# A recurrent transformer's segment loop on one core: transposed scores, sums by a ones matmul, V in two column tiles, memory rows copied per PSUM bank

## The chip, the cores and the metric

The kernel runs on one core of one Trainium2 chip. The metric is the device time of one execution in microseconds (us). The kernel before takes 1736.54 us (median of 3 runs, 1736.03 to 1736.92).

The engines are PE (TensorE, matmuls; PEld is its weight load, which overlaps), DVE (VectorE), ACT (ScalarE), POOL (GpSimd) and SP (SyncE, which issues DMAs). Matmuls write into eight PSUM banks, `pb[0]` to `pb[7]`; DVE or ACT copies the results ("evicts" them) to SBUF. PE can run at a reduced clock; the profile records the clock that was granted, 1.00 being full.

## The reference

The output is a mixture of two models, `g*a + (1-g)*b`, over 2048 tokens of width 512. Model b is a linear-memory attention, which the kernel computes first, in about the first 350 us. Model a is the expensive one. It is recurrent: 64 segments, and each needs the memory that the one before produced.

```python
M, seg, H, Dh = 8, 32, 32, 128          # 8 memory rows, 32 tokens, 32 heads of 128
mask = (idx[:, None] < M) | (idx[:, None] >= idx[None, :])
mem = mem0
for s in range(64):
    h = concatenate([mem, x[:, s*32:(s+1)*32]])           # 40 rows x 512
    q, k, v = h@Wq, h@Wk, h@Wv                            # 32 heads each
    p = softmax(where(mask, q@k.T * scale, -1e9))         # 40 x 40 per head
    o = (p @ v) @ Wo                                      # 40 x 512
    mem = o[:8]                                           # needed by segment s+1
    outs.append(o[8:])
```

No work of segment s+1 that depends on `h` can start before the end of segment s, so the loop is one long chain. Anything in a segment that leaves PE idle is paid 64 times.

## The kernel before

The program is scheduled by hand: each engine executes its instructions in the order in which the Python code puts them out, and semaphores follow from declared reads and writes. `L` = 40 rows, `C` = 4 contraction chunks of 128, `E` = 128, `SEG` = 32. In a segment, tokens stand in columns 0 to 31 and memory rows in columns 32 to 39.

```python
# scores: [q, k] per head, 32 matmuls; exp on ACT, mask on POOL, sum / reciprocal / multiply on DVE
ins = pe.matmul(pb[b][0:L, ...], QT_sb[:, h*L:(h+1)*L], KT_sb[:, h*L:(h+1)*L], start=True, stop=True)
... a.activation(P_sb[0:L, h0:h1, :], pb[b][0:L, ...], ACT.Exp, scale=SCALE)
... g.affine_select(P_sb[0:SEG, h0:h1, 0:SEG], ...)
... dv.tensor_reduce(rsum, P_sb, AX.X, ALU.add); dv.reciprocal(rrec, rsum); dv.tensor_tensor(Pn_sb, P_sb, rrec, ALU.mult)

# P has to be turned for P@V: 32 PE transposes, then a DVE copy
ins = pe.transpose(dst, Pn_sb[0:L, h, :], ident[0:L, 0:L])

# V: 8 groups of 512 columns; the output fills only 40 of 128 PSUM partitions
for c in range(c0, c1):
    ins = pe.matmul(pb[vb][0:L, 0:512], hTc[:, c, :], Wv_sb[:, c, 512*j:512*(j+1)], start=(c == 0), stop=(c == C-1))

seq = [("K",0),("K",1),("K",2),("hx",None),("Q",0),("Q",1),("Q",2),("V",0),("sc",0),("sc",1),("V",1),("sc",2),
       ("V",2),("V",3),("V",4),("ptr",0),("V",5),("V",6),("ptr",1),("V",7),("ptr",2)]
... # then P@V (32 matmuls) into OT_sb, evicted by ACT

# output projection: 128 matmuls into ONE bank, then two DVE copies, one after the other
for c in range(C):
    ... pe.matmul(pb[6][:, c*L:(c+1)*L], Wo_sb[:, h, c*128:(c+1)*128], OT_sb[:, h*L:(h+1)*L], ...)
... dv.tensor_copy(aT_st[...], pb[6] columns 0:SEG)            # tokens, "aT"
... dv.tensor_copy(hTc[:, :, SEG:L], pb[6] columns SEG:L)      # memory rows, "hm": K of the next segment waits for this
```

Every fourth segment a finished block of 128 output rows is combined with model b (`brow`, `atr`, `t1`, `fin`) and sent out; `fin` reads bank 6 too.

The softmax here doesn't subtract the row's maximum and nothing guards it: scores larger than these inputs give would overflow.

## Time and profile before

| what | number | where to read it |
|---|---|---|
| PE busy over the span of 1731.7 us | 89% | page, part 1 |
| PE busy between 1000 and 1700 us | 671.39 of 700 us, clock 0.99 | windows |
| first K matmul of the segment loop | 352.3 us | the line's instructions |
| the loop | 1731.7 - 352.3 = 1379.4 us | |
| distance between memory copies (62 intervals, 382.1 to 1707.1 us) | 21.37 us | the line's instructions |

The page's first part (busy us, share of the span, instructions):

```profile
PE 1547.3 (89%) x37477; PEld 1163.0 (67%) x37573; DVE 725.5 (42%) x1733; ACT 732.3 (42%) x1471; POOL 204.1 (12%) x396
```

That average mixes model b with the loop. The windows view, one stretch of the loop only (from:to in us, its length, busy time of each engine, granted clock, DMA share, GB/s):

```profile
1000.00:1700.00 700.00, 671.39 (x16771) 516.14 (x16801) 271.19 (x607) 271.09 (x524) 60.41 (x131) 0.99 0.02 5
```

So the loop is bound by PE, and every other engine has room. The chain of waits shows what PE does in one plain segment (start us, length us, what; L822 is K and Q, L888 V, L874 the transposes, L937 P@V, L950 the output projection):

```profile
1000.74 0.29 DVE aT_st L956
1001.04 0.11 DVE hT L806
1001.14 0.05 issue
1001.19 6.58 PE pb L822 x256
1007.77 0.97 PE pb L888 x4
...
1010.41 2.60 PE pb L888 x12
1013.01 0.40 PE pb L874 x12
...
1016.91 0.71 PE pb L937 x24
...
1018.06 3.59 PE pb L950 x128
```

The V projection alone is 7.2 of these 20.9 us. The group lines tell why it is worth attacking (line, engine, operation, tiles, shapes, count | busy us, mean ns | idle before it):

```profile
L888 PE MATMUL pb<-Wv_sb,hT 128*40 128x512 bf16 x2048 | 498.7, 381 | 4.3 <-DMA Wv_sb<-in_A_Wv_dram 4.3
L950 PE MATMUL pb<-OT_sb,Wo_sb 128*128 128x40 bf16 x8192 | 235.6, 182 | 16.4 <-DVE fin L1017 16.4
...
L843 PE MATMUL pb<-KT_sb,QT_sb 128*40 128x40 bf16 x2048 | 72.4, 180 | 0.0
```

Read "128*40": 128 rows of the array are used, but only 40 of its 128 columns. The mean of 381 ns is the length of one matmul from start to modelled end; they are pipelined, so the busy time over the count, 498.7 / 2048 = 243 ns, is nearer to what one costs.

Last, the waits of PE (total us, times, longest):

```profile
PE pb L822 <- DVE hT L806: 23.2, 48, 0.5
PE pb L950 <- DVE fin L1017: 16.4, 15, 1.1
PE pb L633 <- DVE phiQ L519: 14.4, 15, 1.1
```

The first is the copy tail at the end of each segment, the second the output combination each fourth segment, the third lies in model b, before the loop.

### The profile page before, as it was taken

How to read it: one execution, taken by the hardware profiler on the slowest of the kernel's cores; microseconds unless marked ns; L12 is line 12 of the kernel's file. 1: busy time of each engine (PE TensorE's matmuls, PEld its weight loads, DVE VectorE, ACT ScalarE, POOL GpSimd, SP SyncE). 2: the span in 40 equal slices, each digit the busy share in tenths (PEclk: the TensorE clock that was granted, in tenths of full speed). 3: DMA queues.
4: the chain of work that ended last, by engine and by line, in shares of the span. 5: the costliest groups of instructions: out<-in, count | busy, mean ns of one | idle time of the engine just before them, and what ended most of it. 6: DMA issues, size and time to landing. Idle time of an engine off the chain costs nothing.

```text
span 1731.7 us, 80136 instructions
## 1 busy us (share of the span) xinstructions
PE 1547.3 (89%) x37477; PEld 1163.0 (67%) x37573; DVE 725.5 (42%) x1733; ACT 732.3 (42%) x1471; POOL 204.1 (12%) x396
## 2 busy tenths in 40 slices
PE   4776666679999999999999999999999999999999
PEld 3444444467777777777777777777777777777776
DVE  3556565533334333334333333333333333333333
ACT  4756464624343434333433333333333333333333
POOL 1322222300000100000000000000000000000000
PEclk8977786679999999999999999999999999999999
DMA  7000000050000000000000000000000000000000
GB/s 292 3 2 2 2 2 2 2 196 4 6 3 6 3 6 3 6 3 6 3 6 3 6 3 7 3 6 3 6 3 6 4 6 3 6 3 6 4 6 6
DMA packets 12916, 28.22 MB, mean 16 GB/s; under 512 B 800, under 2 KB 11048, under 8 KB 11048
## 3 DMA queue, kind: packets, MB, share of 16 engines
q1 hardware_dynamic: 12584, 23.09, 3.6%
q8 instruction: 294, 4.82, 1.1%
q14 instruction: 38, 0.31, 0.1%
HBM read 20.99 MB, written 2.10 MB: 13 GB/s over the span
## 4 chain that ended last, share of the span: by engine, by line
PE 74%; DVE 3%; issue 1%; DMA 1%; SPq 0%
PE pb L888 27%; PE pb L822 24%; PE pb L950 14%; PE pb L874 4%; PE pb L937 3%; PE pb L843 3%; DVE aT_st L956 1%; DMA Wv_sb<-in_A_Wv_dram 1%; DVE fin L1017 1%; DVE t_sb L1013 1%; DVE hT L806 0%; PE pb L971 0%; DVE V_sb L894 0%; DVE PT_sb L878 0%; SPq L304 0%
## 5 line engine op out<-in xcount | busy, mean ns | idle before, releaser
L888 PE MATMUL pb<-Wv_sb,hT 128*40 128x512 bf16 x2048 | 498.7, 381 | 4.3 <-DMA Wv_sb<-in_A_Wv_dram 4.3
L897 ACT ACTIVATE V_sb<-pb 40x512 bf16<-40x512 f32 x448 | 264.8, 591 | 361.2 <-PE pb L888 361.2
L888 PEld LDWEIGHTS pb<-Wv_sb,hT 128*40 128x40 bf16 x2048 | 179.0, 99 | 175.5 <-DMA Wv_sb<-in_A_Wv_dram 4.4
L828 ACT ACTIVATE KT_sb<-pb 128x480 bf16<-128x480 f32 (+1 forms) x192 | 101.1, 527 | 394.9 <-PE pb L822 394.9
L832 DVE CAST QT_sb<-pb 128x480 bf16<-128x480 f32 (+1 forms) x192 | 115.7, 603 | 351.1 <-PE pb L822 343.0
L950 PE MATMUL pb<-OT_sb,Wo_sb 128*128 128x40 bf16 x8192 | 235.6, 182 | 16.4 <-DVE fin L1017 16.4
L950 PEld LDWEIGHTS pb<-OT_sb,Wo_sb 128*128 128x128 bf16 x8192 | 224.5, 97 | 26.0 <-ACT OT_sb L941 17.5
L822 PE MATMUL pb<-hT,Wk_sb 128*128 128x40 bf16 x8192 | 216.7, 180 | 25.1 <-DVE hT L806 23.2
L822 PEld LDWEIGHTS pb<-hT,Wk_sb 128*128 128x128 bf16 x8192 | 210.8, 96 | 28.8 <-DVE hT L806 26.6
L822 PE MATMUL pb<-hT,Wq_sb 128*128 128x40 bf16 x8192 | 216.6, 179 | 1.7 <-issue 1.3
L822 PEld LDWEIGHTS pb<-hT,Wq_sb 128*128 128x128 bf16 x8192 | 210.4, 96 | 2.5 <-issue 2.2
L851 POOL TENSOR_SCALAR_AFFINE_SELECT P_sb<-P_sb 32x384 bf16<-32x384 bf16 (+1 forms) x192 | 98.8, 527 | 936.6 <-ACT P_sb L848 936.6
L595 ACT ACTIVATE PT_g<-pb 128x512 bf16<-128x512 f32 (+1 forms) x384 | 170.5, 529 | 75.7 <-PE pb L586 73.7
L856 DVE TENSOR_REDUCE rsum<-P_sb 40x12 f32<-40x480 bf16 (+1 forms) x192 | 112.0, 584 | 149.7 <-POOL P_sb L851 149.7
L956 DVE CAST aT_st<-pb 128x128 bf16<-128x128 f32 x64 | 18.7, 292 | 263.3 <-PE pb L950 263.3
L941 ACT ACTIVATE OT_sb<-pb 128x480 bf16<-128x480 f32 (+1 forms) x192 | 87.1, 526 | 94.6 <-PE pb L937 94.6
L861 DVE TENSOR_TENSOR Pn_sb<-P_sb,rrec 40x480 bf16<-40x480 bf16 (+1 forms) x192 | 118.9, 619 | 6.6
L874 PEld LDWEIGHTS pb<-ident,Pn_sb 40*40 40x40 bf16 x2048 | 63.5, 93 | 81.0 <-DVE PT_sb L878 27.0
L601 POOL TENSOR_SCALAR_AFFINE_SELECT PT_g<-PT_g 128x512 bf16<-128x512 bf16 x128 | 82.7, 646 | 257.5 <-ACT PT_g L595 255.3
L843 PEld LDWEIGHTS pb<-KT_sb,QT_sb 128*40 128x40 bf16 x2048 | 71.5, 98 | 30.3 <-issue 1.1
L848 ACT ACTIVATE P_sb<-pb 40x480 bf16<-40x480 f32 (+1 forms) x192 | 91.0, 508 | 0.0
L586 PE MATMUL pb<-QTg,KTg 16*128 16x128 bf16 x1280 | 44.6, 253 | 44.4 <-ACT PT_g L595 40.7
(85 smaller groups left out, 1117.1 us busy)
## 6 DMA issues: line engine op xcount, KB each, us to landing
Wk_sb<-in_A_Wk_dram SPq DMA_DIRECT2D x4, 1024.0 KB, 11.7
Wq_sb<-in_A_Wq_dram SPq DMA_DIRECT2D x4, 1024.0 KB, 20.0
Wv_sb<-in_A_Wv_dram SPq DMA_DIRECT2D x4, 1024.0 KB, 9.2
Wo_sb<-in_A_Wo_dram SPq DMA_DIRECT2D x4, 1024.0 KB, 13.8
x_sb<-in_A_x_dram SPq DMA_DIRECT2D x4, 512.0 KB, 5.6
out_dram<-fin SPq DMA_DIRECT2D x16, 128.0 KB, 1.7
wqN_sb<-in_B_wq_dram SPq DMA_DIRECT2D x1, 512.0 KB, 7.8
wkN_sb<-in_B_wk_dram SPq DMA_DIRECT2D x1, 512.0 KB, 8.9
```

The costliest lines, as they stand in the source:

```text
L595: P.op("act", (lambda j=j: (lambda a: a.activation(ptb[:, j, 128 * n0:128 * (n0 + len(wv))], pb[j][:, 0:128 * len(wv)], ACT.Exp, scale=SCA ...
L822: ins = pe.matmul(pb[bnk][:, (h - h0) * L:(h - h0 + 1) * L], wsb[:, c, h * E:(h + 1) * E], hTc[:, c, :], start=(c == 0), stop=(c == C - 1))
L828: P.op("act", (lambda bnk=bnk, dst=dst, h0=h0, h1=h1: (lambda a: a.activation(dst[:, h0 * L:h1 * L], pb[bnk][:, 0:(h1 - h0) * L], ACT.Copy ...
L832: P.op("dve", (lambda bnk=bnk, dst=dst, h0=h0, h1=h1: (lambda dv: dv.tensor_copy(dst[:, h0 * L:h1 * L], pb[bnk][:, 0:(h1 - h0) * L])))(), ...
L843: ins = pe.matmul(pb[b][0:L, (h - h0) * L:(h - h0 + 1) * L], QT_sb[:, h * L:(h + 1) * L], KT_sb[:, h * L:(h + 1) * L], start=True, stop=True)
L851: P.op("gp", (lambda h0=h0, h1=h1, nh=nh: (lambda g: g.affine_select(P_sb[0:SEG, h0:h1, 0:SEG], P_sb[0:SEG, h0:h1, 0:SEG], [[0, nh], [-1, ...
L856: P.op("dve", (lambda h0=h0, h1=h1: (lambda dv: dv.tensor_reduce(rsum[0:L, h0:h1], P_sb[0:L, h0:h1, :], AX.X, ALU.add)))(), reads=[rP], wr ...
L861: P.op("dve", (lambda h0=h0, h1=h1, nh=nh: (lambda dv: dv.tensor_tensor(Pn_sb[0:L, h0:h1, :], P_sb[0:L, h0:h1, :], rrec[0:L, h0:h1].unsque ...
L874: ins = pe.transpose(dst, Pn_sb[0:L, h, :], ident[0:L, 0:L])
L888: ins = pe.matmul(pb[vb][0:L, 0:512], hTc[:, c, :], Wv_sb[:, c, 512 * j:512 * (j + 1)], start=(c == 0), stop=(c == C - 1))
L897: P.op("act", (lambda vb=vb, j=j: (lambda a: a.activation(V_sb[0:L, 512 * j:512 * (j + 1)], pb[vb][0:L, 0:512], ACT.Copy)))(), reads=[rban ...
L950: ins = pe.matmul(pb[6][:, c * L:(c + 1) * L], Wo_sb[:, h, c * 128:(c + 1) * 128], OT_sb[:, h * L:(h + 1) * L], start=(h == 0), stop=(h == ...
```

## The change

The intent: use the idle columns of the array for V, get rid of the transposes, and hide the copy tail.

- Heads are ordered in pairs. V is written to two column tiles, partitions 0 to 39 and 64 to 103 of the same bank, by two matmuls that can run side by side. Each eviction then moves 104 partitions, so there are 4 instead of 8.
- Scores are computed as [k, q], in the same two column tiles. P is then already turned for P@V. The sum over k now runs over partitions, so it is done by a matmul with a block matrix of ones. The reciprocal is `Exp(-Ln(sum))` on ACT, the mask a multiply by 0 and 1 on DVE.
- The output projection goes half by half of the heads into two banks; the memory rows of the first bank are copied while PE works on the second, and the first group of K starts with the two contraction chunks that are ready first.
- The output combination moves under K. In model b the `nz` matmuls, which read its memory `MZ` with the queries `phiQ`, are put out before the Q projection.

The diff, cut to its core:

```diff
-            for c in range(c0, c1):
-                ins = pe.matmul(pb[vb][0:L, 0:512], hTc[:, c, :], Wv_sb[:, c, 512 * j:512 * (j + 1)],
+            for c in range(C):
+                for g2 in range(2):
+                    n0 = g2 * HS * E + 512 * j
+                    ins = pe.matmul(pb[j][64 * g2:64 * g2 + L, 0:512], hTc[:, c, :], Wv_sb[:, c, n0:n0 + 512],
...
-                ins = pe.matmul(pb[b][0:L, ...], QT_sb[:, h * L:(h + 1) * L], KT_sb[:, h * L:(h + 1) * L], ...)
+                ins = pe.matmul(pb[6 + t // HB_][64 * g2:64 * g2 + L, ...],
+                                KT_sb[:, p * L:(p + 1) * L], QT_sb[:, p * L:(p + 1) * L], ...)
...
+    def softmax_norm(i):
+        P.op("pe", lambda pe: pe.matmul(pb[4 + i][:, 0:W], onesg[0:NP, :], P_sb[0:NP, i * W:(i + 1) * W], ...
+        P.op("act", ... a.activation(R_sb[...], pb[4 + i][0:NP, 0:W], ACT.Ln) ...
+        P.op("act", ... a.activation(R_sb[...], R_sb[...], ACT.Exp, scale=-1.0) ...
+        P.op("dve", ... dv.tensor_tensor(Pn_sb[...], P_sb[...], R_sb[...], ALU.mult) ...
...
+    vproj(0)
+    scores(0, 16)
+    scores(16, 32)
+    softmax_exp(0)
+    softmax_exp(1)
+    vproj(1)            # evicted by ACT
+    softmax_norm(0)
+    vproj(2)            # evicted by ACT
+    softmax_norm(1)
+    vproj(3)            # evicted by DVE
+    pv(0)
+    pv(1)
+    for c in range(C):
+        wo(0, c)        # first half of the heads, banks 4 and 5
+    wo(1, 0)
+    wo(1, 1)
+    tail(0, False)      # memory rows of bank 4
+    tail(0, True)       # tokens of bank 4
+    wo(1, 2)
+    wo(1, 3)
+    tail(1, False)
+    tail(1, True)
...
+        if havep:
+            seq.append(("nz", None))
         if haven:
             seq.append(("pQ", None))
...
-            seq.append(("nz", None))
```

## The prediction

> **What bounds it now.** TensorE (PE) in the segment loop. The window table gives PE busy 671.4 of 700 us between 1000 and 1700 us (96%), clock 0.99; VectorE and ScalarE are each at 39%. The loop runs from about 353 us to the end (1379 us). The memory copies into hT (382.1 to 1707.1 us) give 21.37 us a segment. The chain of waits for one plain segment (1000.74 to 1021.67 us, 20.93 us) is nearly all PE: K and Q projections 6.6, V projection 7.25 (32 matmuls of 512 columns, 226 ns each), output projection 3.6, probability transposes 1.1, PV 1.15, scores 0.8, and 0.43 us of copies (aT, then hT) before the next K. Each fourth segment waits another 1.1 us for fin.
>
> **What the change does on PE, per segment.**
> - V in two column tiles: 32 matmuls in 16 pairs that can overlap. The Trainium skill, "TensorE: Matmul & The Clock Gate", Part 3, reports 2.38x for three column tiles. This trace agrees in kind: the column-tiled MZ update takes 19 ns a matmul of 32 columns, the untiled MZ read 36 ns. Estimate 115 to 120 ns a matmul, V 3.8 us: -3.4 us.
> - Transposed scores make the transposes needless: -1.1. Two ones matmuls of 320 columns: +0.3. [...]
> - PV as row-tile pairs: -0.4. Scores as column pairs: -0.2.
> - Memory rows copied per bank, and K group 0 split by contraction half: the 0.43 us tail is hidden. fin moves under K1, K2: -0.27 on average.
>
> Sum: about 16 us of PE work.
>
> **What it adds on the chain.** Softmax now passes exp, mask (VectorE), ones matmul, Ln, Exp(-1), multiply. With a 320-column ScalarE op at 0.44 us, 512-column evictions at 0.59 and 0.68, and a VectorE multiply at about 0.45, laid out in each engine's program order, the second half's reciprocal ends only after vev1, ln0, rex0, vev2, ln1, rex1 in the ScalarE queue. The last V eviction stands behind the second multiply, so the second PV starts about 1.7 to 2.1 us after PE has finished the first. The first half's output projection is planned only after the second PV. So I expect 18.1 us a segment, not 16. The instruction order shows no table load between Exp and Ln.
>
> **Attention part before.** The nz matmuls wait 14.4 us in all for phiQ (waits, PE). Moved ahead of the Q projection they should not wait, and fill waits for phiKg (9.5 us). I take -10 us.
>
> **Sum.** Segments: 64 x (21.37 - 18.1) = -209; attention -10; setup hides under the wait for Wv (4.3 us). 1736.5 - 219 = 1517 us; range 1450 to 1600. Faster by over 2%: 0.97; within 2%: 0.02; slower: 0.01.
>
> **What the profile would show.** V matmul starts at about 115 ns mean spacing (right) or 220 (wrong: then some 20.4 us a segment, 1665 us). The wait before PV: one per segment, 1.5 to 2.1 us, released by VectorE (V eviction or Pn). The wait before K0 gone. No transposes, no masks on GpSimd. The nz wait near 0, the segment loop starting about 10 us earlier.
>
> **What would make it wrong.** (1) Column tiles do not overlap. (2) The granted clock: it is 0.6 to 0.8 in the attention part, where PE waits often; a 2 us hole a segment might bring it below 0.99 and cost up to 10% of the loop. (3) The softmax chain is shorter (bf16 mask multiply near 0.3 us, semaphore hops small) or longer by 1 us: 64 us either way.

## The result and the profile after

The changed kernel takes 1479.63 us (median of 4 runs, 1472.42 to 1483.17), against 1736.73 us (1736.03 to 1737.02) for the one before in the same job. The ratio is 0.8517, with a 95% interval of 0.8493 to 0.8541: about 15% faster. Here and below, a ratio is the mean time of one kernel's fast runs over that of the other's of the same rounds, so it is not quite the ratio of the medians quoted. Different jobs ran on different chips, so differences between experiments are taken from the ratios: a difference of 0.001 is 1.74 us.

Page, part 1, of the kernel after:

```profile
PE 1251.3 (85%) x35605; PEld 980.8 (66%) x35653; DVE 621.3 (42%) x1542; ACT 579.6 (39%) x1280; POOL 106.1 (7%) x212
```

PE's share fell from 89% to 85%: PE got less to do, and it also waits more. The windows view of the loop shows 91% busy and a clock below 1:

```profile
420.00:1000.00 580.00, 526.29 (x15916) 425.50 (x15920) 218.95 (x511) 193.83 (x428) 9.98 (x33) 0.95 0.02 6
```

The chain of waits through one plain segment (L840 is K and Q, L859 V, L885 scores, L918 P@V, L943 the output projection; L865 and L868 evict V, L902 is Ln, L904 Exp, L906 the multiply):

```profile
1000.30 6.55 PE pb L840 x256
...
1008.22 0.89 PE pb L859 x8
1009.11 0.02 issue
1009.13 0.60 ACT V_sb L865
1009.73 0.34 ACT R_sb L902
...
1010.09 0.47 ACT R_sb L904
1010.55 0.49 ACT V_sb L865
1011.04 0.34 ACT R_sb L902
...
1011.40 0.48 ACT R_sb L904
...
1011.90 0.49 DVE Pn_sb L906
1012.39 0.61 DVE V_sb L868
1013.00 0.14 issue
1013.14 0.38 PE pb L918 x16
```

In the middle of the segment the chain has left PE. From 1009.13 to 1013.00 it goes through six ACT operations in ACT's program order, then the multiply, then the last V eviction, which stands behind that multiply on DVE. The waits of PE give the price:

```profile
PE pb L918 <- DVE V_sb L868: 84.1, 64, 1.3
...
PE pb L840 <- issue: 11.8, 25, 1.7
...
PE pb L943 <- issue: 4.1, 8, 1.2
```

One wait per segment, 1.31 us each, 84.1 us in all. The waits for the memory copy, for `fin` and for phiQ are gone. The groups:

```profile
L859 PE MATMUL pb<-Wv_sb,hT 128*40 128x512 bf16 x2048 | 268.2, 383 | 2.0 <-DMA Wv_sb<-in_A_Wv_dram 2.0
L943 PE MATMUL pb<-OT_sb,Wo_sb 128*128 128x40 bf16 x8192 | 244.6, 188 | 9.4 <-issue 4.1 <-DMA Wo_sb<-in_A_Wo_dram 3.7
...
L885 PE MATMUL pb<-QT_sb,KT_sb 128*40 128x40 bf16 x2048 | 37.0, 180 | 0.0
```

This is a lesson in reading groups: the V matmul's mean length is unchanged (381 and 383 ns), and only the busy time, 498.7 to 268.2 us, tells that two now run at once. The scores halved likewise (72.4 to 37.0).

One plain segment, by the starts of PE's runs in the timelines of both kernels:

| part of the segment | before, us | after, us | difference |
|---|---|---|---|
| K and Q | 6.51 | 6.65 | +0.14 |
| V | 7.22 | 3.80 | -3.42 |
| scores | 0.82 | 0.40 | -0.42 |
| transposes / ones matmuls | 1.10 / none | none / 0.48 | -0.62 |
| P@V, with the wait inside it | 1.19 | 2.08 (0.77 + 1.31) | +0.89 |
| output projection | 3.61 | 3.98 | +0.37 |
| copies before the next K | 0.48 | 0 | -0.48 |
| sum | 20.93 | 17.39 | -3.54 |

Over the whole program, the first K matmul comes at 339.0 us instead of 352.3 (-13.3), and the loop takes 1141.2 us instead of 1379.4 (-238.2); together that is the difference of the spans, 251.5 us. The memory copies (366.2 to 1457.2 us, 62 intervals) are 17.60 us apart.

One row has the wrong sign: the output projection has the same 128 matmuls, and takes longer. The granted clock explains it. Windows view of PE around this segment's hole (stretch, length, PE busy, granted clock, DMA share, GB/s):

```profile
1010.50:1013.50 3.00, 1.69 (x41) 1.00 0.00 0
1014.50:1017.50 3.00, 3.00 (x97) 0.50 0.02 5
```

The hole itself is at full clock. Just after it, with PE fully busy, the clock is one half for 3.41 us. The trace has 36 such stretches after 370 us, the last of them behind the last matmul. Before the change there were 12, the last of them likewise; the other 11 begin during one of the 15 waits for `fin` (1.1 us) or at most 1.5 us after it.

The segment shown is one that was hit. Over all 64, from the first matmul of the output projection to the next work of PE, the median is 3.97 us in the 36 segments whose output projection meets a half-clock stretch and 3.25 us in the other 28: less than the 3.61 before. So the half clock costs 36 x 0.72, or about 26 us, in this row. The stretches of the loop all begin on one grid of 3.413 us, to within 2 ns, while the holes come every 17.6 us; whether a hole is followed by one may depend on where it falls on that grid, which no run tests.

### The profile page after: what moved, and what is told of

Its sections match the earlier page's. It is cut to its first block, busy times and chain, and to the rows that moved or that the text cites. A ratio compares the mean times of both kernels' runs of the same rounds, so it can differ in the third digit from the quotient of the medians.

```text
span 1480.2 us, 75277 instructions
## 1 busy us (share of the span) xinstructions
PE 1251.3 (85%) x35605; PEld 980.8 (66%) x35653; DVE 621.3 (42%) x1542; ACT 579.6 (39%) x1280; POOL 106.1 (7%) x212
## 4 chain that ended last, share of the span: by engine, by line
PE 57%; ACT 12%; DVE 5%; issue 2%; SPq 1%; DMA 1%
PE pb L840 28%; PE pb L943 17%; PE pb L859 8%; ACT V_sb L865 5%; ACT R_sb L904 4%; ACT R_sb L902 3%; DVE V_sb L868 3%; DVE Pn_sb L906 2%; PE pb L885 2%; PE pb L918 2%; PE pb L1008 1%; DMA Wo_sb<-in_A_Wo_dram 1%; SPq L310 1%; PE pb L1016 0%; SPq L304 0%
## 5 line engine op out<-in xcount | busy, mean ns | idle before, releaser
L859 PE MATMUL pb<-Wv_sb,hT 128*40 128x512 bf16 x2048 | 268.2, 383 | 2.0 <-DMA Wv_sb<-in_A_Wv_dram 2.0
L943 PE MATMUL pb<-OT_sb,Wo_sb 128*128 128x40 bf16 x8192 | 244.6, 188 | 9.4 <-issue 4.1
L943 PEld LDWEIGHTS pb<-OT_sb,Wo_sb 128*128 128x128 bf16 x8192 | 238.3, 101 | 15.3 <-issue 8.7
L840 PE MATMUL pb<-hT,Wk_sb 128*128 128x40 bf16 x8192 | 224.5, 181 | 7.8 <-issue 5.0
L840 PE MATMUL pb<-hT,Wq_sb 128*128 128x40 bf16 x8192 | 220.2, 180 | 7.5 <-issue 6.8
L840 PEld LDWEIGHTS pb<-hT,Wk_sb 128*128 128x128 bf16 x8192 | 217.4, 97 | 9.2 <-issue 9.0
L840 PEld LDWEIGHTS pb<-hT,Wq_sb 128*128 128x128 bf16 x8192 | 212.3, 96 | 10.0 <-issue 9.5
L892 ACT ACTIVATE P_sb<-pb 104x320 bf16<-104x320 f32 x128 | 49.0, 434 | 271.5 <-PE pb L885 271.5
L859 PEld LDWEIGHTS pb<-Wv_sb,hT 128*40 128x40 bf16 x2048 | 85.2, 99 | 81.2 <-issue 3.5
L906 DVE TENSOR_TENSOR Pn_sb<-P_sb,R_sb 104x320 bf16<-104x320 bf16 x128 | 63.0, 492 | 140.6 <-ACT R_sb L904 140.6
L918 PE MATMUL pb<-Pn_sb,V_sb 40*128 40x40 bf16 x2048 | 47.6, 178 | 84.1 <-DVE V_sb L868 84.1
L918 PEld LDWEIGHTS pb<-Pn_sb,V_sb 40*128 40x128 bf16 x2048 | 36.0, 93 | 116.0 <-ACT OT_sb L927 89.0
L988 DVE CAST hT<-pb 128x16 bf16<-128x16 f32 x126 | 22.0, 174 | 199.5 <-PE pb L943 199.5
L868 DVE CAST V_sb<-pb 104x512 bf16<-104x512 f32 x128 | 88.0, 687 | 33.5 <-PE pb L859 33.5
L927 ACT ACTIVATE OT_sb<-pb 128x320 bf16<-128x320 f32 x128 | 56.0, 437 | 79.8 <-PE pb L918 79.7
L865 ACT ACTIVATE V_sb<-pb 104x512 bf16<-104x512 f32 x128 | 75.3, 588 | 17.5 <-PE pb L859 17.4
```

What stands on the lines that cost most here:

```text
L840: ins = pe.matmul(pb[bnk][:, (p - h0) * L:(p - h0 + 1) * L], wsb[:, c, h * E:(h + 1) * E], hTc[:, c, :], start=(c == 0 and (p == h0 or not ...
L859: ins = pe.matmul(pb[j][64 * g2:64 * g2 + L, 0:512], hTc[:, c, :], Wv_sb[:, c, n0:n0 + 512], start=(c == 0), stop=(c == C - 1))
L865: P.op("act", lambda a: a.activation(V_sb[0:NP, 512 * j:512 * (j + 1)], pb[j][0:NP, 0:512], ACT.Copy), reads=[rbank[j]], writes=[rv], name ...
L868: P.op("dve", lambda dv: dv.tensor_copy(V_sb[0:NP, 512 * j:512 * (j + 1)], pb[j][0:NP, 0:512]), reads=[rbank[j]], writes=[rv], name="vev%d ...
L906: P.op("dve", lambda dv: dv.tensor_tensor(Pn_sb[0:NP, i * W:(i + 1) * W], P_sb[0:NP, i * W:(i + 1) * W], R_sb[0:NP, i * W:(i + 1) * W], AL ...
L918: ins = pe.matmul(pb[2 * i + g2][:, (t % HB_) * L:(t % HB_ + 1) * L], V_sb[p0:p0 + L, t * E:(t + 1) * E], Pn_sb[p0:p0 + L, t * L:(t + 1) * L],
```

## The experiments

Eleven kernels were run. All edits are on the kernel after. All results are correct except where stated.

### e1: the nz matmuls back in their old place

```diff
-        if havep:
-            seq.append(("nz", None))
         if haven:
             seq.append(("pQ", None))
...
+            seq.append(("nz", None))
         if haven:
             seq.append(("pV", None))
```

> The changed kernel with the nz matmuls put back behind the last PV part (their old place, which also reads phiQ too late again, so the numbers change slightly). Theory: the move was worth about 14 us (the segment loop began at 339.0 us after the change and at 352.3 us before it, by the first K matmul), so this run is 10 to 16 us slower than the changed kernel (near 1491 to 1496 us), its first K matmul is near 352 us, and the wait of nz for phiQ is back at about 14 us. Rival: the earlier loop start came from elsewhere or is noise; then the first K matmul stays near 339 us.

Measured: 1489.24 us (1486.1 to 1491.38), ratio 0.8598 (0.8569 to 0.8627). That is 0.0081 more than the change, 14 us. The first K matmul came at 352.8 us instead of 339.0, and the loop took 1131.6 us (10 us less than in the profiled run of the change, whose own runs scatter over 11 us). The wait is back:

```profile
PE pb L631 <- DVE phiQ L517: 14.8, 15, 1.1
```

So the move alone accounts for the 13.3 us gained before the loop. It was predicted at 10, because I thought that other waits would take up some of the 14.4.

### e2: V column tiles not alternating in the program

If PE starts matmuls in program order, side-by-side work needs the two tiles to alternate. Here the four matmuls of one tile come first, then the four of the other.

```diff
-            for c in range(C):
-                for g2 in range(2):
+            for g2 in range(2):
+                for c in range(C):
```

> Same matmuls, same column tiles, but all four of one tile first and then all four of the other, so neighbours can no longer overlap. Theory: the gain in V comes from neighbours in different column tiles running at once; then V goes from about 120 ns to about 226 ns a matmul start to start, 3.4 us of PE work more per segment, of which the wait before the second PV hides up to 1 us: 2.3 to 3.2 us a segment, 1625 to 1685 us in all. Rival: the gain comes from the column-tile mode itself, or from 104-partition evictions (4 in place of 8); then the order does not matter and the time stays within 1% of 1480 us.

Measured: 1477.46 us (1476.12 to 1479.47), ratio 0.8527 (0.8502 to 0.8552): no difference. I expected most of the gain to be lost, so this was a plain miss. The group line is the old one:

```profile
L859 PE MATMUL pb<-Wv_sb,hT 128*40 128x512 bf16 x2048 | 270.7, 382 | 2.1 <-DMA Wv_sb<-in_A_Wv_dram 2.1
```

The starts of one group of eight in the trace are 1004.136, .159, .351, .374, .566, .589, .781 and .804 us: four pairs, 23 ns within a pair, 215 ns between pairs. In the change itself the pairs are 4 ns apart, every 215 ns. So PE ran the two tiles as two streams side by side, though the program lists one after the other. The records do not name the tile of a matmul, so this is inferred from the pairs; the trace of e2b, below, shows it by line.

### e2b: V matmuls alternating, but in one and the same column tile

This separates "the other tile" from "the order". Both halves accumulate into partitions 0 to 39, which gives a wrong result (relative error 1.2), and all eight banks are zeroed once at the start, not shown in the cut. All other sizes stay.

```diff
-                    ins = pe.matmul(pb[j][64 * g2:64 * g2 + L, 0:512], hTc[:, c, :], Wv_sb[:, c, n0:n0 + 512],
-                                    start=(c == 0), stop=(c == C - 1))
+                    ins = pe.matmul(pb[j][0:L, 0:512], hTc[:, c, :], Wv_sb[:, c, n0:n0 + 512],
+                                    start=(c == 0 and g2 == 0), stop=(c == C - 1 and g2 == 1))
```

> All eight V matmuls of a bank in the SAME column tile (partitions 0 to 39); the result is wrong on purpose, counts and sizes are the same. Theory after e2: the order in the program does not matter, because PE runs the two tiles as two streams; what matters is that there are two tiles. Then V takes about 216 to 226 ns a matmul here (7 us a segment in place of 3.8), of which the wait before the second PV hides up to 1 us: 2.2 to 3.2 us a segment, 1620 to 1685 us. Rival: V is faster only since it is evicted in four 104-partition pieces and never waits for a bank; then the time stays near 1480 us.

Measured: 1627.31 us (1622.33 to 1629.48), ratio 0.9361 (0.9344 to 0.9377), as expected. Its V group, then its wait at P@V:

```profile
L859 PE MATMUL pb<-Wv_sb,hT 128*40 128x512 bf16 x2048 | 486.5, 380 | 0.0
```

```profile
PE pb L918 <- ACT OT_sb L927: 36.6, 64, 0.6
```

V's busy time is back, +218 us, but the kernel lost only 0.0844 against the change, or 147 us. The rest is given back elsewhere: with V slow, PE's wait at P@V is 0.57 us a segment instead of 1.31 (-47.5 us in all), and the loop's clock is 1.00, which e5 below puts at about 26 us; 218 - 47.5 - 26 is 145. So the tiles relieve PE by 3.4 us a segment, but shorten the segment by only some 2.3 us in this schedule, because a faster V leaves less time in which to hide the softmax.

This trace also settles what e2 left to inference. The scores still alternate between the two tiles, and the program puts them after all eight matmuls of the first V bank, which are now in the first tile alone. The timeline of one segment, weight loads left out:

```profile
1011.13 1.47 PE L859 MATMUL pb<-Wv_sb,hT 128*40 128x512 bf16 x6
...
1012.23 0.20 PE L885 MATMUL pb<-QT_sb,KT_sb 128*40 128x40 bf16 x1
1012.44 0.38 PE L859 MATMUL pb<-Wv_sb,hT 128*40 128x512 bf16 x1
```

A score matmul starts before the last two V matmuls that stand ahead of it in the program. In all 64 segments two scores start before the last V matmul of that bank, the first of them 0.42 us (median) ahead of it.

### e3 and e3b: the copies after the whole output projection

In e3 the first group of K is not split, and the copies come after all of the output projection, memory rows first. In e3b the token copies come first, as before the change.

```diff
-        early = kind == "K" and b == 0
+        early = False
...
-    tail(0, False)
-    tail(0, True)
     wo(1, 2)
     wo(1, 3)
+    tail(0, False)          # e3b: tail(0, True), tail(1, True), tail(0, False), tail(1, False)
     tail(1, False)
+    tail(0, True)
     tail(1, True)
```

> Both memory copies only after the whole output projection, and K group 0 in one piece that waits for both. Theory: the split hides the PE idle of about 0.5 us a segment that the kernel before had in front of K; undone, the wait for hT in front of K0 is back at 0.45 to 0.65 us a segment and the time is 29 to 42 us longer (1509 to 1522 us). Rival: the split was worth little, because the wait before the second PV is the only slack that matters; then under 10 us.

> As e3, but with the two copies to aT ahead of the two memory copies on VectorE, the order that the kernel before had. Theory: e3 lost only 0.27 us a segment since it kept the memory copies first; the kernel before lost 0.48 us since aT came first. The wait of K for hT is then 0.40 to 0.55 us a segment. Rival: the copy order does not matter and the wait stays at 0.27 us.

Measured, e3: 1486.41 us (1484.01 to 1492.47), ratio 0.8583 (0.8552 to 0.8614), so 0.0066 or 11 us slower, against 29 to 42 expected: a miss. Measured, e3b (one run, state unknown): 1516.52 us, 0.874 of the median before in the same job, about 38 us slower. Their waits before K, in this order:

```profile
PE pb L840 <- DVE hT L988: 16.9, 63, 0.3
```

```profile
PE pb L840 <- DVE hT L988: 34.7, 63, 0.6
```

The tail is 0.55 us a segment with the old order of copies, 0.27 with the memory rows first, and 0 with the copies per bank. By these waits, half of the gain comes from the mere order of the copies, and the other half from the split. In e3, moreover, the waits that the profile calls "issue" fell from 15.9 to 5.7 us, so that even the 16.9 us did not arrive in full.

### e4: scores not alternating in the program

The same question as e2, with short matmuls: eight of one tile, then eight of the other.

```diff
-            for p in range(p0, p1):
+            for p in list(range(p0, p1, 2)) + list(range(p0 + 1, p1, 2)):
```

> Score matmuls of one column tile together (eight, then eight) in place of alternating. Theory: alternating tiles is why a score matmul takes 12.5 ns start to start (32 in 0.40 us) and not 25 ns as before the change; grouped they take about 25 ns, 0.4 us a segment more, and as the softmax chain hangs on them all of it shows: 20 to 28 us longer (1500 to 1508 us). Rival: a matmul of 40 columns is bound by issue or weight load whatever the tile; then no change.

Measured: 1487.71 us (1479.03 to 1489.52), ratio 0.8575 (0.854 to 0.861): 10 us slower by the ratios, with an uncertainty of some 7 us, against 20 to 28 expected.

```profile
L885 PE MATMUL pb<-QT_sb,KT_sb 128*40 128x40 bf16 x2048 | 47.0, 181 | 0.1
```

The group rose from 37.0 to 47.0 us; fully serial it was 72.4. The starts of one segment, from the first, are 0, 28, 53, 78, 103, 109, 128, 150, 153, 175, ... 446, 471, 496, 521, 546 ns. The first few stand alone at 25 ns, then a second stream joins, and at the end the rest stands alone again. So here too matmuls of different column tiles overlap out of program order, but the second stream starts only when its first matmul is four places behind the one just started: the reach is a few matmuls. For V's groups of four that is far enough (e2), for scores in eights it is not.

### e5 and e5b: the hole filled with useless matmuls

Does the idle hole cause the half clock? Useless matmuls are put between the two halves of P@V, into bank 6, which is free then. In e5 they are five of 512 columns, in e5b 44 of 40 columns.

```diff
     pv(0)
+    def f_fill(pe):
+        for i in range(NFILL):       # e5: 5, N = 512; e5b: 44, N = 40
+            ins = pe.matmul(pb[6][0:L, 0:N], hTc[:, i % C, :], Wv_sb[:, i % C, 0:N], start=True, stop=True)
+        return ins
+    P.op("pe", f_fill, ...)
     pv(1)
```

> The changed kernel with five useless V-shaped matmuls of 512 columns (about 1.1 us of PE work) after the first PV, in the place where PE waits 1.3 us a segment; their result is never read. Theory: the half-clock stretches of 3.4 us that follow some of these waits (36 of them in the loop of the changed kernel) come from the wait itself; with PE kept busy they vanish, the mean clock in the loop goes from 0.95 to 0.98 or more, an output projection takes 3.6 us again and not 4.0, and the kernel is 8 to 18 us FASTER in spite of more work; the spread of its runs falls below 3 us. Rival: the stretches come from something else in the segment; then the clock stays near 0.95 and the time is the same or longer.

> As e5, but the hole is filled with 44 useless matmuls of 40 columns (about 1.1 us, 88 PE instructions with their weight loads) in place of five of 512 columns (10 instructions). Theory after e5: the PE waits called issue stand at multiples of 256 PE instructions and end about 1.4 us after a 16 KB instruction fetch has landed, so PE is now at times limited by the supply of instructions; 78 more instructions a segment and no pause before the dense stretch of output, K and Q projections make these waits longer: from 31 us in e5 to 45 us or more, and the kernel is 10 to 30 us slower than e5 (1484 to 1504 us), with the clock in the loop still at 0.98 or more. Rival: these waits do not depend on the number of instructions; then the time is that of e5, 1471 to 1478 us.

Measured, e5: 1474.25 us (1473.25 to 1475.91), ratio 0.8485 (0.8473 to 0.8497), while the unchanged kernel in the same job had 0.8515 (0.8495 to 0.8535). Adding work made it 0.003, or 5 us, faster, with an uncertainty of some 4 us. The loop's window:

```profile
420.00:1000.00 580.00, 559.50 (x16283) 431.46 (x16289) 219.65 (x514) 195.37 (x431) 9.67 (x33) 1.00 0.02 6
```

The clock is 1.00, and the output projection's busy time fell from 244.6 to 221.7 us. That part of the theory stands: the holes cause the half clock, and it costs about 23 us in the output projection and 3 in K, which agrees with the 26 us that the segments of the change itself gave. The total gain was smaller than that (and below the 8 to 18 us expected), because of the waits:

```profile
PE pb L841 <- issue: 22.0, 49, 1.6
PE pb L944 <- issue: 8.7, 17, 0.9
```

They rose from 15.9 to 30.7 us. The sum: 26 us less of half clock, 15 us more of these waits, and a filler that takes 4.6 us more than the hole did (80.4 us busy and 8.3 us of idle behind it, against 84.1) leave 6 us.

What are they? In the trace of e5, each of these 66 pauses in K, Q and the output projection stands a multiple of 256 PE instructions after the one before (65 of 65, to within two) and, but for one, ends 1.2 to 1.6 us, in the median 1.4, after a DMA of 16,384 bytes of instructions landed. PE waited for its own program. My theory then was that the rate depends on how many instructions are executed in the time, and e5b, with 88 instructions of filler a segment instead of 10, should have been slower than e5. It was faster: 1464.42 us (1462.07 to 1465.13), ratio 0.8434 (0.8418 to 0.8451), with 19.3 us of such waits instead of 30.7. That theory fell. What sets how often PE waits for instructions stays open. The totals differ even between near copies of the kernel (5.7 us in e3, 10.9 in e1, 12.2 in e4, 13.1 in e2, 15.9 in the change).

### a0: the same kernel again

This run measures the unchanged kernel beside e5 and the others in the same job.

> The changed kernel once more, as the reference of this call on this chip: 1472 to 1483 us, half-clock stretches in about half of the segments (mean granted clock near 0.95 in the loop).

Measured: 1473.65, 1481.55, 1483.03 and 1480.52 us, and once 5152.58 us; ratio of the fast runs 0.8515 (0.8495 to 0.8535), so the first result repeats. In the slow run, which was the profiled one, the mean V matmul was 1621 ns instead of 383, while the granted clock was recorded as 1.000. It is left out of all comparisons, and nothing is explained by it.

### e7: the reciprocal on DVE

Is the Ln and Exp pair on ACT, which makes up most of the chain through the hole, a bad choice?

```diff
-        P.op("act", ... a.activation(R_sb[...], pb[4 + i][0:NP, 0:W], ACT.Ln) ...
-        P.op("act", ... a.activation(R_sb[...], R_sb[...], ACT.Exp, scale=-1.0) ...
+        P.op("dve", ... dv.reciprocal(R_sb[...], pb[4 + i][0:NP, 0:W]) ...
```

> VectorE reciprocal of the 320 column sums in place of Ln and Exp(-1) on ScalarE. Estimate from the kernel before: a reciprocal of 128x16 takes 0.255 us where a multiply of the same size takes 0.175, so about 5 ns more per column, some 1.7 us for 320 columns. Theory: the softmax chain becomes longer than with Ln and Exp (0.90 us together), the wait before the second PV grows by 1 to 2 us, 1540 to 1610 us. Rival: reciprocal runs[...] like the other VectorE operations (0.5 us); then the chain is shorter and the kernel 20 to 40 us faster.

Measured (one run, state unknown): 1647.6 us, 0.949 of before, about 170 us slower than the change. One reciprocal of 320 columns takes 2.15 us, where Ln and Exp together take 0.90:

```profile
L902 DVE RECIPROCAL R_sb<-pb 104x320 f32<-104x320 f32 x128 | 275.7, 2154 | 10.1 <-PE pb L900 2.8
```

```profile
PE pb L916 <- DVE V_sb L868: 180.7, 64, 2.8
PE pb L916 <- DVE Pn_sb L904: 43.2, 64, 0.7
```

The waits before P@V grew from 84 to 224 us, and the loop's clock fell to 0.85. The direction was as expected, the size larger (1540 to 1610 expected): I had put the reciprocal at 1.7 us, and I had left out the clock.

### e8: the segment rescheduled so that no hole arises

The chain through the hole is only an order of operations on ACT and DVE, so it can be changed. Both ones matmuls come after V1; V1 is evicted by DVE; both Ln and Exp pairs run ahead of V2's eviction on ACT; the first half of P@V goes into the middle of V3, and three quarters of the first half's output projection run ahead of the second P@V.

```diff
     vproj(1)
-    softmax_norm(0)
+    sm_sum(0)
+    sm_sum(1)
     vproj(2)
-    softmax_norm(1)
-    vproj(3)
-    pv(0)
-    pv(1)
-    for c in range(C):
+    sm_rec(0)                 # Ln, Exp on ACT
+    sm_rec(1)
+    vproj(3, 0, 2)            # first two contraction chunks
+    sm_mul(0)
+    pv_mm(0)
+    pv_ev(0)
+    vev(2)
+    vproj(3, 2, C)
+    sm_mul(1)
+    vev(3)
+    for c in range(3):
         wo(0, c)
+    pv_mm(1)
+    pv_ev(1)
+    wo(0, 3)
     wo(1, 0)
```

> A schedule meant to close the wait before the second PV: both ones matmuls straight after V1, the V1 eviction on VectorE, both reciprocals ahead of the V2 eviction on ScalarE, the first PV between the halves of V3, and three quarters of the first half's output projection ahead of the second PV. Theory: the wait of 1.3 us falls to 0.2 to 0.5 us a segment (now in front of the output projection), and the half-clock stretches go with it: 60 to 90 us faster than the changed kernel, 1390 to 1420 us. Rival: the chain is the limit wherever the work is put; then the wait moves in front of the output projection at full length and the gain is under 20 us.

Measured: 1407.57 us (1400.37 to 1412.75), ratio 0.8095 (0.8071 to 0.8118). This beats both kernels; it is 0.042 or 73 us below the change in the same job. The wait for P@V has left the list of waits, and the clock is full:

```profile
PE pb L840 <- issue: 17.9, 40, 1.8
...
PE pb L955 <- DVE OT_sb L942: 10.9, 63, 0.2
```

```profile
420.00:1000.00 580.00, 555.70 (x17022) 444.67 (x17026) 252.96 (x578) 189.23 (x420) 14.06 (x35) 1.00 0.02 6
```

Of the hole's 84.1 us, 10.9 come back as a new, short wait of the output projection for the eviction of P@V's result. The output projection became only 4 us shorter (244.6 to 240.6), although the clock is full, probably because it now runs in two stretches; that was not tested. The sum, 84.1 - 10.9 + 4.0 = 77 us, is within the scatter of the 73 measured.

## Why the prediction was right

The time, 1479.63 us, lies in the predicted range of 1450 to 1600, some 37 us below the predicted 1517. The mechanisms hold, point by point; three sizes were off.

- **What bounded it** was right: PE, in the loop. The V busy time, the transposes and the tail all turned into time.
- **V in two tiles, -3.4 us a segment** (115 to 120 ns a matmul): measured -3.42 us, 3.80 us for 32 matmuls, 119 ns each. e2b shows that the second tile is the cause. The reason given, "pairs that can overlap", was too narrow: e2 shows that pairs next to each other in the program are not needed.
- **Transposes -1.1, ones matmuls +0.3, P@V -0.4**: measured -1.10, +0.48, and -0.42 for the matmuls of P@V without the wait. These are read from the traces; no run undoes them one by one.
- **Scores -0.2**: measured -0.42, mis-sized. Two short matmuls start in 25 ns, where one did.
- **The wait before the second P@V, 1.7 to 2.1 us, released by VectorE**: the place, the releaser and the chain of operations (two V evictions, two Ln and two Exp on ACT, the multiply, the last eviction) are as predicted; the size is 1.31 us. This is the largest of the mis-sized terms, 0.4 to 0.8 us a segment or 25 to 50 us in all. ACT's six operations add up to 2.98 us by their own records but took 2.75 us, from 1009.13 to 1011.88, since three of them start 0.1 us before the record of the last ends; and the last V eviction starts 0.08 us before the record of the multiply ends. That is 0.3 us; for the rest I have no single cause.
- **The tail hidden, -0.43, and fin, -0.27**: both waits are gone (23.2 and 16.4 us in all). e3 and e3b show that half of the tail would have gone by merely copying the memory rows first.
- **Attention part, -10**: measured -13.3, and e1 shows that it is all due to moving the nz matmuls.
- **The named risk, that the hole would lower the clock**: it did, from 0.99 to about 0.95. e5 puts its cost at about 26 us, 2% of the loop, where up to 10% had been feared. Half clock costs little here: the output projection takes 3.97 us with it and 3.25 without, in the same trace.

Two terms were left out. Before, the output projection's first weights also waited for the last part of P@V's result, 17.5 us in all for PEld, which the change removes. And PE now waits for its instructions, 15.9 us against 1.8 in the loop before.

That the time came so near to 1517 is partly luck: the wait taken too long (25 to 50 us), the scores taken too slow and the weights' wait left out point one way, and the half clock (about 26 us) and the waits for instructions (14 us more than before), neither of them in the sum, point the other.

The sums: predicted -3.27 us a segment, measured 21.37 - 17.60 = -3.77.

## What to carry to other kernels

Halving the matmul time of a stage halves the time in which another engine's chain can hide, so lay out that chain in each engine's program order before counting the gain; here the chain took back 1.3 us a segment, and a new order of the same operations (e8) won a further 73 us. A narrow output (40 of 128 columns) is worth putting into two column tiles even when the code cannot alternate them perfectly, but it pays to alternate short matmuls. Short idle holes had a second price here, in the clock after them, so look at the granted clock after a hole, not in it.

## What the Trainium skill lacked or had wrong

- "TensorE: Matmul & The Clock Gate", Part 3, "The mechanism", says that matmuls start and end in program order, with no reordering. Across two column tiles that is not what the trace shows: e2 lists four V matmuls of one tile, then four of the other, and they start as pairs 23 ns apart every 215 ns; e4 shows the same for scores, with a reach of a few matmuls; and in e2b, in all 64 segments, scores of one tile start ahead of V matmuls of the other (0.42 us) that precede them in the program. "TensorEngine Tiling (Array Packing)", Key Properties, says that tiles operate independently, which agrees.
- The same Part 3 gives 2.38x for three column tiles; for two tiles of 64 columns no page has a measured figure, only a theoretical one. Here two tiles took a V matmul of 512 columns from 7.22 / 32 = 226 ns to 119 ns, 1.9x.
- "TensorE: Matmul & The Clock Gate", "Why this matters for your kernels", asks for no idle gaps above about 3 us; its section "A second HAM failure mode: psum-queue depth-cycling" says that frequent micro-idles can do it too, without a size. Here holes of 1.31 us, one each 17.6 us, gave 35 half-clock stretches of 3.41 us within the loop after 370 us (the length agrees with the window that Part 1 states), and filling them gave a clock of 1.00. In e2b, holes of 0.57 us gave 1.00; in e7, 2.8 and 0.7 us gave 0.85.
- "Runtime: NRT & Kernel Launch", Instruction fetch mechanics, calls the cost of crossing a block of 256 instructions mostly hidden. Here PE, in dense stretches, waited 5.7 us (e3) to 30.7 us (e5) for instructions, in e5 always a multiple of 256 PE instructions apart (65 of 65), up to 1.7 us at once in the change. What sets the frequency stays open.
- "VectorE: DVE Perf Modes", "Walkthrough: the 8-slice pipeline in each mode", says that the reciprocal is an iterative divide, but gives no duration. Here 320 columns took 2.15 us, 6.7 ns a column, against 0.90 us for Ln and Exp on ACT.
